# Converting weight blocks in pairs, and a new order of the opening, in a fused attention and two-layer kernel

## The chip, the cores and the metric
The kernel runs on one core of a Trainium2 chip. The metric is device microseconds (us) of one execution, as a median of runs; smaller is better. The engines are TensorE (PE in the profile; its weight loads are PEld), VectorE (DVE), ScalarE (ACT), GpSimd (POOL) and SyncE (SP), which here only issues transfers (DMA). Each engine works through its own list of instructions strictly in the order in which the program lays them down, and waits at an instruction whose inputs aren't there yet.

## The reference, cut to what matters
```python
# attention: 4 batches, 8 heads, 576 positions, 64 per head; position i sees i-63 .. i
scores = scale * q @ k.T ; scores[outside window] = -1e9 ; attn = softmax(scores) ; o = attn @ v
x = o as 2304 tokens x 512
# first layer: w_in 512 x 2048, w_out 2048 x 512
g = softplus(x @ w_in) ; x2 = g @ w_out
# second layer: w_gate, w_val 512 x 1536, w_out 1536 x 512
y = (sigmoid(x2 @ w_gate) * (x2 @ w_val)) @ w_out
```
The weights arrive in double precision.

## The kernel before, in words
Queries are taken in groups of 64 positions (36 groups, 9 per batch); a group needs 128 keys, two neighbouring blocks of 64. Tokens go through the first layer in five blocks of 512, 384, 384, 512 and 512. Block 0 consists of groups 0 to 7, called near; their whole attention has to be done before the first projection (`m1_proj`, tile `h<-xt,w`) can start. I call the time up to that first projection the opening. Later groups' attention is slipped in between the projections of the block before theirs.

Every fp32 matmul of the two layers is made of three passes over a high and a low part (`mm3`, lines 349 to 351 before). So each block of weights, 128 x 512 values, has to be turned from the raw double bits into such a pair: `w_load` (SP, 512 KB), `w_scale` (ACT, L115), `w_shift`, `w_sign`, `w_low` (DVE, L120, L124, L129), `w_hi` (ACT, L135, writes the high part) and `w_lo` (POOL, L140, the difference). The first layer has 32 such blocks (16 of `w1`, 16 of `w2`), which are converted during the opening and block 0 and then stay in 32 slots `w0` to `w31`. The blocks of `wg` and `wv` are converted next, summed and split (`c_sums`, `c_hi`, `c_lo`) and sent back to memory (`c_send`) for the second layer; I call one wg block with its wv block a combination. There are 12. The 12 blocks of `wo` come last.

The attention of a group: `att_scores` (PE, L250), `att_max` (DVE, L259, L262), `att_exp` (ACT, L274, four exponentials with their sums), `att_sum` (DVE, L279, L280), `att_norm` (POOL, L285), `att_transpose` (PE, L293), `att_copy` (ACT, L322), `att_values` (PE, L331), `att_hi` (ACT, L339) and `att_lo` (DVE, L344), which write the block's input `xt`. For the near groups before, queries and keys are loaded apart: each even group takes its keys from the tiles of its two neighbours, by two half-wide matmuls per pair of heads.

The order of everything up to the second layer comes from a planner, `lead_in`: each step has a rank (a slot of the matmul sequence with small offsets), an engine, a duration and the steps that it depends on (`traits`), and the planner goes through a list of engines' free times and lays down what can start first, by rank among those within `SLACK`. In it a load is taken to land 0.85 us after the bytes before it and its own have passed. After the projection of each chunk come softplus (`m1_act`, ACT, L368), `g_hi` (ACT, L375) and `g_lo` (DVE, L381), and then the output matmuls (`m1_out`, tile `acc<-g,w`). Softplus and the exponential need different tables on ACT; changing costs an `ACT_TABLE_LOAD`.

Of the kernel before, what the change touches and what calls it, by code (L numbers as in the profile page):

```python
# [28 lines left out]
FLYING, SWITCH = 10, 1.3  # L29
AHEAD = 160  # L30
STB, PB, VB, GB, RB, BB = 3, 2, 2, 3, 3, 3
# [3 lines left out]
def tile_kernel(ctx: ExitStack, tc: tile.TileContext, qk, vt, w1, w2, wg, wv, wo, out):  # L35
# [68 lines left out]
    raw_t, bits_t, w_t = {}, {}, {}  # L104

    def w_load(i):
        t = main.tile([P, 2 * DM], U32, tag="raw", name="raw", bufs=RB)
        nc.sync.dma_start(out=t, in_=allw[i][1])
        raw_t[i] = t.rearrange("p (n two) -> p n two", two=2)
# [3 lines left out]
    def w_scale(i):  # L113
        t = main.tile([P, DM], U32, tag="bits", name="bits", bufs=BB)
        nc.scalar.activation(out=t.bitcast(F32), in_=raw_t[i][:, :, 1].bitcast(F32), func=AF.Copy, scale=2.0 ** -112)  # L115
        bits_t[i] = t
# [5 lines left out]
    def w_sign(i):  # L122
        t, r = bits_t[i], raw_t[i]
        nc.vector.scalar_tensor_tensor(out=t, in0=r[:, :, 1], scalar=0x80000000, in1=t, op0=ALU.bitwise_and,  # L124
                                       op1=ALU.bitwise_or)

    def w_low(i):
        t, r = bits_t[i], raw_t.pop(i)
        nc.vector.scalar_tensor_tensor(out=t, in0=r[:, :, 0], scalar=29, in1=t, op0=ALU.logical_shift_right,  # L129
                                       op1=ALU.bitwise_or)  # L130

    def w_hi(i):
        t, slot = bits_t[i].bitcast(F32), place[i]
        w = wpool.tile([P, 2, DM], F32R, tag=f"w{slot}", name=f"w{slot}", bufs=1)
        nc.scalar.copy(out=w[:, 0, :], in_=t)  # L135
        w_t[allw[i][0]] = w

    def w_lo(i):
        t, w = bits_t.pop(i).bitcast(F32), w_t[allw[i][0]]
        nc.gpsimd.tensor_tensor(out=w[:, 1, :], in0=t, in1=w[:, 0, :].bitcast(F32), op=ALU.subtract)  # L140
# [5 lines left out]
    def c_load(i):  # L146
        w_load(i)
        send_t[i] = raw_t[i].rearrange("p n two -> p (n two)").bitcast(F32R).rearrange("p (e n) -> p e n", e=2)

    def c_sums(f):  # L150
        g, v = (bits_t[len(seq1) + 2 * f + k].bitcast(F32) for k in range(2))
        x = main.tile([P, DM], F32, tag="bits", name="sums", bufs=BB)
        a11, a12, a21, a22, s1, s2 = (t[:, k * HC:(k + 1) * HC] for t in (g, v, x) for k in range(2))
        nc.vector.tensor_tensor(out=s1, in0=a21, in1=a22, op=ALU.add)
        nc.vector.tensor_tensor(out=s2, in0=s1, in1=a11, op=ALU.subtract)
        nc.vector.tensor_tensor(out=a21, in0=a11, in1=a21, op=ALU.subtract)
        sum_t[f] = x

    def c_sum4(f):
        g = bits_t[len(seq1) + 2 * f].bitcast(F32)  # L160
        nc.vector.tensor_tensor(out=g[:, HC:], in0=g[:, HC:], in1=sum_t[f][:, HC:], op=ALU.subtract)

    def c_part(f, part):
        i = len(seq1) + 2 * f
        if part == "x":
            t = sum_t[f]
            if (f, part) not in send_t:
                r = main.tile([P, 2 * DM], U32, tag="raw", name="sumr", bufs=RB)
                send_t[f, part] = r.bitcast(F32R).rearrange("p (e n) -> p e n", e=2)
            return t, send_t[f, part], 4 * DM  # L170
        if part == "s4":
            t = bits_t[i]
            return t.bitcast(F32)[:, HC:], t.bitcast(F32R).rearrange("p (e n) -> p e n", e=2), 6 * DM
        k = "av".index(part)
        return bits_t[i + k].bitcast(F32), send_t[i + k], 2 * k * DM
# [5 lines left out]
    def c_lo(f, part):  # L181
        t, o, _ = c_part(f, part)
        nc.gpsimd.tensor_tensor(out=o[:, 1, :], in0=t, in1=o[:, 0, :].bitcast(F32), op=ALU.subtract)
# [25 lines left out]

    def v_load(g):  # L210
        b, i = divmod(g, NSEQ)
        c0, c1 = max(i - 1, 0) * Q, (i + 1) * Q
        if g < NG0:
            vp = wpool.tile([P, 2, DM], F32, tag=f"w{NSLOT - 1 - NG0 - g}", name="vp0", bufs=1)
            v, p_t[g] = vp[:, 0, :], vp[:, 1, :].rearrange("p (j k) -> p j k", j=NPAIR)
# [6 lines left out]
    def first_tile(g):  # L222
        if g not in qk_t:
            qk_t[g] = wpool.tile([P, 2, NPAIR, P], F32, tag=f"w{NSLOT - 1 - g}", name="qk0", bufs=1)
        return qk_t[g]

    def q_load(g):
        nc.sync.dma_start(out=first_tile(g)[:, 0], in_=qk[g, :, 0])

    def k_load(t):  # L230
        nc.sync.dma_start(out=first_tile(2 * t + 1)[:, 1], in_=qk[2 * t + 1, :, 1])

    def qk_load(g):
        t = late["apool"].tile([P, 2, NPAIR, P], F32, tag="qk", name="qk", bufs=2)
# [3 lines left out]
    def att_scores(g):  # L238
# [3 lines left out]
        if g >= NG0 or g % 2:  # L242
            parts = [(0, w, t[:, 1])]
        elif g:
            parts = [(0, Q, qk_t[g - 1][:, 1, :, Q:]), (Q, Q, qk_t[g + 1][:, 1])]
        else:
            parts = [(0, Q, qk_t[1][:, 1])]
        for j in range(NPAIR):
            for at0, n, keys in parts:
                nc.tensor.matmul(out=s[:, j, at0:at0 + n], lhsT=t[:, 0, j, :], rhs=keys[:, j, :n], start=True,  # L250
                                 stop=True)
        s_t[g] = s

    def att_max(g):
        w = width(g)
        s = s_t.pop(g)
        p = p_t[g] if g < NG0 else late["apool"].tile([P, NPAIR, P], F32, tag="p", name="p", bufs=PB)
# [169 lines left out]
    def x2_hi(s, k, kc):  # L427
        c = wpool.tile([P, 2, DM], F32R, tag=f"w{2 * k + kc}", name="xc", bufs=1)[:, :, :HALF]
# [9 lines left out]
    def tmp(s, f, k):  # L438
        if (s, f, k) not in tmp_t:
            i = (s * NF2 + f) % 2  # L440
            t = wpool.tile([P, 2, DM], F32, tag=f"w{NSLOT - NF2 - 6 + 3 * i + k}", name=f"t{k}", bufs=1)
# [151 lines left out]
    def weight(i, t):  # L593
        at(t - 2, 50, w_load, i)
# [5 lines left out]
        at(t + 2, -19, w_lo, i)  # L600

    for i in range(len(seq1)):
# [4 lines left out]
    def used_last(slot):  # L607
        (kind, f), _ = seq1[slot]
        return pos[m1_proj if kind == "w1" else m1_out, NB1 - 1, f]

    for f in range(NF2):
        t, i = COMBO0 + int(COMBO * f), len(seq1) + 2 * f
        for k in range(2):
            at(t - 2 + k, -60, c_load, i + k)
            at(t + k, -20, w_scale, i + k)
            at(t + k + 1, -20, w_shift, i + k)
            at(t + k + 1, -19, w_sign, i + k)
            at(t + k + 1, -18, w_low, i + k)
# [6 lines left out]
    for f in range(NF2):  # L625
# [3 lines left out]
        assert used_last(place[i]) < t + 4 < pos[m2_out, 0, f, 0]  # L629
# [43 lines left out]
    for g in range(NG0):  # L673
        t = int(first + RG * g)
        attention(g, t, False)
        if g % 2 == 0:
            at(t - 4, -63, k_load, g // 2)
        at(t - 4, -62, q_load, g)
# [12 lines left out]
    def traits(fn, a, *rest):  # L691
        early = fn.__name__.startswith(("att", "v_")) and a < NG0
        f = rest[-1] if rest else a
        wide = 1.0 if fn.__name__.startswith(("att", "v_")) and width(a) == P else 0.6
        if fn in (w_load, c_load):
            freed = (w_low, a) if fn is w_load else (c_send, (a - NSLOT) // 2, "av"[a % 2])
            f = (a - NSLOT) // 2 - 1
            deps = [(w_load, NSLOT - 1)] if f == -1 else [(c_hi, f, "x")] if f >= 0 else []
            return "sp", 512, deps * (fn is c_load or a == WO_AT), [("raw", RB, freed)]
        if fn is qk_load:  # L700
            return "sp", 512, [], [("qk", 2, (att_scores, a))]
# [208 lines left out]
```

## Time and profile before
| what | us |
|---|---|
| median of 3 runs (944.41 to 946.98) | 945.0 |
| profiled execution, whole | 943.91 |
| its span, first to last instruction | 942.1 |
| PE busy in the span | 898.3 (95%) |
| DVE, ACT, POOL busy | 512.0, 401.4, 251.1 |

The profiled execution's time is 1.81 us over its span. PE is the engine that sets the end: its busy time, with the weight loads beside it, is 95% of the span. The 43.8 us in which it is not busy, and the stretches in which its clock is granted at half, are what a better order can give back. The clock of the span's first 15 us is not in the record and is shown as full there; durations of single matmuls tell more in that stretch.

### The profile page before, as it was taken

How to read it: one execution, taken by the hardware profiler on the slowest of the kernel's cores; microseconds unless marked ns; L12 is line 12 of the kernel's file. 1: busy time of each engine (PE TensorE's matmuls, PEld its weight loads, DVE VectorE, ACT ScalarE, POOL GpSimd, SP SyncE). 2: the span in 40 equal slices, each digit the busy share in tenths (PEclk: the TensorE clock that was granted, in tenths of full speed). 3: DMA queues.
4: the chain of work that ended last, by engine and by line, in shares of the span. 5: the costliest groups of instructions: out<-in, count | busy, mean ns of one | idle time of the engine just before them, and what ended most of it. 6: DMA issues, size and time to landing. Idle time of an engine off the chain costs nothing.

```text
span 942.1 us, 13708 instructions
## 1 busy us (share of the span) xinstructions
PE 898.3 (95%) x5024; PEld 805.2 (85%) x5024; DVE 512.0 (54%) x922; ACT 401.4 (43%) x928; POOL 251.1 (27%) x232
## 2 busy tenths in 40 slices
PE   6589998899999998999999899999999999999998
PEld 6468877899889987888888799998999998999996
DVE  3787877465556565654211558666545446444443
ACT  4767666563766566543312332334222224222222
POOL 2443344232232222231100223334211114111111
PEclk9899999999999999999999999999999999999999
DMA  9445654866777576674002656554564444644441
GB/s 325 141 149 179 206 178 142 267 214 219 267 250 271 209 261 201 216 263 169 1 1 101 246 205 237 188 208 166 219 232 169 163 158 163 218 157 157 157 157 67
DMA packets 56643, 176.54 MB, mean 187 GB/s; under 512 B 6144, under 2 KB 21248, under 8 KB 51968
## 3 DMA queue, kind: packets, MB, share of 16 engines
q1 hardware_dynamic: 56576, 175.66, 53.2%
q8 instruction: 40, 0.66, 0.3%
q14 instruction: 27, 0.22, 0.1%
HBM read 138.67 MB, written 36.96 MB: 186 GB/s over the span
## 4 chain that ended last, share of the span: by engine, by line
PE 76%; DMA 7%; DVE 7%; ACT 4%; issue 3%; POOL 1%; SPq 1%; ACTq 0%; DVEq 0%; POOLq 0%
PE h L349 14%; PE h L350 14%; PE h L351 14%; PE acc L351 9%; PE acc L349 9%; PE acc L350 9%; DMA raw<-in_wv 2%; PE at L250 2%; DMA wcd<-raw 2%; PE at L351 1%; DVE t L457 1%; PE at L350 1%; PE at L349 1%; PE at L331 1%; DMA qk<-in_qk 1%
## 5 line engine op out<-in xcount | busy, mean ns | idle before, releaser
L457 DVE TENSOR_TENSOR t<-h,t 128x384 f32<-128x384 f32 x216 | 117.0, 556 | 169.1 <-PE h L351 160.9
L349 PE MATMUL h<-xc,wc 128*128 128x384 f32 x504 | 170.1, 337 | 1.3 <-DVE t L457 0.9
L350 PE MATMUL h<-xc,wc 128*128 128x384 f32 x504 | 170.4, 338 | 0.0
L351 PE MATMUL h<-xc,wc 128*128 128x384 f32 x504 | 169.8, 337 | 0.0
L463 POOL TENSOR_TENSOR g<-t,g 128x384 fp32r<-128x384 f32 x72 | 74.5, 1035 | 297.9 <-ACT g L462 297.9
L349 PE MATMUL h<-xt,w 128*128 128x512 f32 (+1 forms) x320 | 120.7, 377 | 11.6 <-DVE g L381 10.2
L349 PE MATMUL acc<-g,w 128*128 128x512 f32 (+1 forms) x320 | 120.6, 377 | 2.6 <-ACT w L135 2.6
L381 DVE TENSOR_TENSOR g<-h,g 128x512 fp32r<-128x512 f32 (+1 forms) x80 | 50.7, 635 | 132.1 <-ACT g L375 131.9
L351 PE MATMUL acc<-g,w 128*128 128x512 f32 (+1 forms) x320 | 119.1, 372 | 1.2 <-POOL w L140 1.2
L351 PE MATMUL h<-xt,w 128*128 128x512 f32 (+1 forms) x320 | 118.4, 370 | 0.8 <-POOL w L140 0.8
L350 PE MATMUL h<-xt,w 128*128 128x512 f32 (+1 forms) x320 | 118.4, 370 | 0.5 <-DVE xt L344 0.5
L350 PE MATMUL acc<-g,w 128*128 128x512 f32 (+1 forms) x320 | 118.6, 371 | 0.0
L349 PEld LDWEIGHTS h<-xc,wc 128*128 128x128 f32 x504 | 95.1, 189 | 10.7 <-DVE t L457 1.9
L462 ACT CAST g<-t 128x384 fp32r<-128x384 f32 x72 | 37.0, 514 | 156.6 <-DVE t L457 139.7
L350 PEld LDWEIGHTS h<-xc,wc 128*128 128x128 f32 x504 | 95.1, 189 | 6.5
L140 POOL TENSOR_TENSOR w<-bits,w 128x512 fp32r<-128x512 f32 x44 | 59.4, 1352 | 136.7 <-ACT w L135 84.2
L351 PEld LDWEIGHTS h<-xc,wc 128*128 128x128 f32 x504 | 95.2, 189 | 0.0
L368 ACT ACTIVATE h<-h 128x512 f32<-128x512 f32 (+1 forms) x80 | 43.2, 540 | 112.5 <-PE h L351 112.3
L349 PEld LDWEIGHTS h<-xt,w 128*128 128x128 f32 x320 | 60.5, 189 | 21.0 <-DVE g L381 11.6
L115 ACT ACTIVATE bits<-raw 128x512 f32<-128x512 f32 x68 | 45.4, 671 | 63.4 <-DMA raw<-in_wv 22.8
L349 PEld LDWEIGHTS acc<-g,w 128*128 128x128 f32 x320 | 60.9, 190 | 11.5 <-ACT w L135 3.5
L351 PEld LDWEIGHTS acc<-g,w 128*128 128x128 f32 x320 | 60.7, 190 | 9.9 <-POOL w L140 2.1
(93 smaller groups left out, 1520.3 us busy)
## 6 DMA issues: line engine op xcount, KB each, us to landing
wc<-wcd SPq DMA_DIRECT2D x36, 1792.0 KB, 7.3
raw<-in_w SPq DMA_DIRECT2D x32, 512.0 KB, 3.8
qk<-in_qk SPq DMA_DIRECT2D x28, 512.0 KB, 4.6
wcd<-raw SPq DMA_DIRECT2D x24, 512.0 KB, 3.8
v<-in_vt SPq DMA_DIRECT2D x25, 256.0 KB, 3.6
raw<-in_wg SPq DMA_DIRECT2D x12, 512.0 KB, 4.6
raw<-in_wv SPq DMA_DIRECT2D x12, 512.0 KB, 4.8
wcd<-sumr SPq DMA_DIRECT2D x12, 512.0 KB, 5.6
```

What stands on the lines that cost most here:

```text
L115: nc.scalar.activation(out=t.bitcast(F32), in_=raw_t[i][:, :, 1].bitcast(F32), func=AF.Copy, scale=2.0 ** -112)
L140: nc.gpsimd.tensor_tensor(out=w[:, 1, :], in0=t, in1=w[:, 0, :].bitcast(F32), op=ALU.subtract)
L250: nc.tensor.matmul(out=s[:, j, at0:at0 + n], lhsT=t[:, 0, j, :], rhs=keys[:, j, :n], start=True, stop=True)
L331: nc.tensor.matmul(out=o[h * Q:(h + 1) * Q, j, :], lhsT=v[:w, (2 * j + h) * Q:(2 * j + h + 1) * Q], rhs=pt[:w, h, j], start=True, stop=True)
L349: nc.tensor.matmul(out=o, lhsT=lh, rhs=rh, start=first, stop=False)
L350: nc.tensor.matmul(out=o, lhsT=lh, rhs=rl, start=False, stop=False)
L351: nc.tensor.matmul(out=o, lhsT=ll, rhs=rh, start=False, stop=last)
L368: nc.scalar.activation(out=t, in_=t, func=AF.Softplus)
L381: nc.vector.tensor_tensor(out=g[:, 1, :n], in0=t, in1=g[:, 0, :n].bitcast(F32), op=ALU.subtract)
L457: nc.vector.tensor_tensor(out=out, in0=a, in1=b, op=op)
L462: nc.scalar.copy(out=g[:, 0, :HALF], in_=t)
L463: nc.gpsimd.tensor_tensor(out=g[:, 1, :HALF], in0=t, in1=g[:, 0, :HALF].bitcast(F32), op=ALU.subtract)
```

## The change
It has four parts.

1. Two neighbouring blocks (2u, 2u+1) are converted by one instruction per step: `w_scale`, `w_shift`, `w_sign`, `w_low` and `w_hi` now work on 128 x 1024 values. Only `w_lo` stays per block, and it may go to POOL or to DVE, whichever the planner sees done first (`EITHER`); so may `c_lo`. The blocks of `wo` stay single.
2. Slots become pairs (`w0` to `w15`, each two of the old). Raw bits and the values in work of most pairs of the first layer lie in slots whose weights come later (`raw_slot`, `bits`), instead of in three small buffers each.
3. Near groups load queries and all 128 keys at once (`qk_load`, 512 KB per group, 4 MB in all instead of 3 MB), and each has four matmuls of full width (64 keys for group 0).
4. The planner: ranks are in microseconds; those of the near attention and of the first layer's weights are worked back from when the matmul that uses them is due; a load is taken to land 1.5 us later than before (`MARGIN`); a table change counts as work of ACT; loads keep their order.

```diff
+OPEN = 34.0
+FLYING, SWITCH, MARGIN = 10, 1.3, 1.5
+EITHER, HALVES = (("pool", 1.29), ("dve lock", 0.69)), (("pool", 0.75), ("dve lock", 0.42))
-STB, PB, VB, GB, RB, BB = 3, 2, 2, 3, 3, 3
+STB, PB, VB, GB, RB = 3, 2, 2, 3, 2
...
+    def raw_slot(u):
+        return u + 4 if u < 4 else u % 4 + 10 if u < 12 and u % 4 > 1 else None
...
+    def bits(i):
+        if i not in bits_t:
+            u, n = i // 2, size(i)
+            if u < 3:
+                t = main.tile([P, 2, DM], U32, tag="g", name="bits", bufs=GB)
+            elif 4 <= u < 14:
+                slot = 14 + u % 4 // 2 if u < 12 else 15
+                t = pair(2 * slot, -20 - u // 2, U32, 2 * DM)[:, u % 2].rearrange("p (c n) -> p c n", c=2)
+            else:
+                t = main.tile([P, 2, DM], U32, tag="bits", name="bits", bufs=1)
...
     def w_scale(i):
-        nc.scalar.activation(out=t.bitcast(F32), in_=raw_t[i][:, :, 1].bitcast(F32), func=AF.Copy, scale=2.0 ** -112)
+        nc.scalar.activation(out=bits(i).bitcast(F32), in_=raw(i, 1).bitcast(F32), func=AF.Copy, scale=2.0 ** -112)
...
-    def w_lo(i):
-        t, w = bits_t.pop(i).bitcast(F32), w_t[allw[i][0]]
-        nc.gpsimd.tensor_tensor(out=w[:, 1, :], in0=t, in1=w[:, 0, :].bitcast(F32), op=ALU.subtract)
+    def w_lo(i, engine):
+        w = w_t[allw[i][0]]
+        t = bits_t[i - i % size(i)][:, i % size(i)].bitcast(F32)
+        eng = nc.gpsimd if engine == "pool" else nc.vector
+        eng.tensor_tensor(out=w[:, 1], in0=t, in1=w[:, 0].bitcast(F32), op=ALU.subtract)
...
     def qk_load(g):
-        t = late["apool"].tile([P, 2, NPAIR, P], F32, tag="qk", name="qk", bufs=2)
+        if g < NG0:
+            t = pair(NSLOT - NG0 + g, -1, F32, 2, NPAIR, P)[:, g % 2]
+        else:
+            t = late["apool"].tile([P, 2, NPAIR, P], F32, tag="qk", name="qk", bufs=2)
...
         for j in range(NPAIR):
-            for at0, n, keys in parts:
-                nc.tensor.matmul(out=s[:, j, at0:at0 + n], lhsT=t[:, 0, j, :], rhs=keys[:, j, :n], start=True,
-                                 stop=True)
+            nc.tensor.matmul(out=s[:, j, :w], lhsT=t[:, 0, j, :], rhs=t[:, 1, j, :w], start=True, stop=True)
...
+            if near or fn.__name__.startswith("w_") and a < NSLOT:
+                if fn is att_lo:
+                    due[key] = min(due.get(key, OPEN), OPEN - 2.9 * (NG0 - 1 - a))
+                us = 2 + us / 400 if kind == "sp" else us + 0.1
+                nodes[key][0] = due[key] - us
...
-                done[key] = dma + 0.85
+                done[key] = dma + 0.85 + MARGIN
```

ACT, from its first exponentials on (`vp` and `w_114` to `w_126` hold near groups' probabilities, `bits<-raw` is `w_scale`, `pt` is `att_copy`, `xt` is `att_hi`). Before:

```order
L274 ACTIVATE vp_129,st<-vp_129,st 128x64 x4
L115 ACTIVATE bits<-raw 128x512
L274 ACTIVATE vp_136,st<-vp_136,st 128x128 x4
L274 ACTIVATE vp_140,st<-vp_140,st 128x128 x4
L322 COPY pt<-acc_211 64x512
L274 ACTIVATE vp_142,st<-vp_142,st 128x128 x4
L115 ACTIVATE bits<-raw 128x512 x2
```

and now:

```order
L297 ACTIVATE w_114,st<-w_114,st 128x64 x4
L297 ACTIVATE w_114,st<-w_114,st 128x128 x4
L297 ACTIVATE w_120,st<-w_120,st 128x128 x4
L345 COPY pt<-acc_176 64x512
L345 COPY pt<-acc_201 128x512
L297 ACTIVATE w_120,st<-w_120,st 128x128 x4
L362 CAST xt<-at 128x4x64 x2
```

No `w_scale` stands among the first groups' exponentials any more; the first one now follows the exponentials of group 6.

SP, the loads from the middle of the opening on (`vp`, `w_126` and `w_197` by L254 are values of near groups, `in_w` are weight blocks). Before:

```order
L218 DMA vp_129<-in_vt 64x512
L231 DMA qk_131<-in_qk 128x512
L228 DMA qk_133<-in_qk 128x512
L228 DMA qk_131<-in_qk 128x512
L218 DMA vp_136<-in_vt 128x512
L108 DMA raw<-in_w 128x1024
L218 DMA vp_140<-in_vt 128x512
```

and now:

```order
L127 DMA w_158<-in_w 128x1024 x2
L254 DMA w_126<-in_vt 128x512
L254 DMA w_197<-in_vt 128x512 x2
L127 DMA w_228<-in_w 128x1024 x2
L127 DMA w_255<-in_w 128x1024 x2
L127 DMA w_297<-in_w 128x1024 x2
L254 DMA v<-in_vt 128x512
```

The first weight block was load 15 and is now load 16, but all eight near groups' keys and queries and two later groups' stand ahead of it, and weight loads come two by two.

ACT at the first projections (`h_520`, `h_539` before and `h_465`, `h_487`, `h_518` now are the first chunks; `p` are probabilities of groups 8 and 9; `w_508`, `w_504` and the like are weights, written by `w_hi`). Before:

```order
L274 ACTIVATE p,st<-p,st 128x128 x4
L274 ACTIVATE p,st<-p,st 128x64 x4
L135 CAST w_552<-bits 128x512
L115 ACTIVATE bits<-raw 128x512
L368 ACT_TABLE_LOAD
L368 ACTIVATE h_520<-h_520 128x512
L375 CAST g<-h_520 128x512
L368 ACTIVATE h_539<-h_539 128x512
```

and now:

```order
L391 ACTIVATE h_465<-h_465 128x512
L398 CAST g<-h_465 128x512
L168 CAST w_504<-bits 128x2x512
L391 ACTIVATE h_487<-h_487 128x512
L297 ACT_TABLE_LOAD
L297 ACTIVATE p,st<-p,st 128x128 x4
L297 ACTIVATE p,st<-p,st 128x64 x4
L398 CAST g<-h_487 128x512
L391 ACT_TABLE_LOAD
L391 ACTIVATE h_518<-h_518 128x512
L168 CAST w_560<-bits 128x2x512
L168 CAST w_568<-bits 128x2x512
```

The exponentials of groups 8 and 9 moved from ahead of the first softplus to behind the second, at the price of two more table loads, and the third and fourth pair's `w_hi` stand behind them.

## Rows read from the trace of the kernel before

**Rows 1.** Windows: stretch, busy us by engine (instructions), mean granted clock, DMA share, GB/s.
```profile
0.00:46.28 46.28, 29.97 (x264) 27.07 (x265) 27.13 (x57) 26.73 (x93) 15.02 (x23) 0.89 0.68 231
46.28:60.00 13.72, 9.94 (x34) 7.53 (x35) 11.75 (x20) 9.87 (x27) 6.13 (x5) 0.88 0.58 197
110.00:160.00 50.00, 45.29 (x227) 35.71 (x227) 35.82 (x58) 35.04 (x79) 21.41 (x16) 0.97 0.49 162
160.00:300.00 140.00, 131.47 (x925) 127.21 (x924) 78.80 (x162) 81.99 (x212) 40.12 (x36) 1.00 0.72 244
300.00:500.00 200.00, 197.53 (x1059) 167.62 (x1058) 91.43 (x168) 92.22 (x206) 43.26 (x39) 0.99 0.48 162
```

**Rows 2.** Waits of PE over the span: total us, times, longest.
```profile
PE h L349 <- DVE g L381: 10.2, 4, 3.3
PE acc L349 <- ACT w L135: 3.6, 3, 1.7
```

**Rows 3.** Timeline of ACT in the opening: start, us, [idle before <-releaser].
```profile
15.66 0.67 ACT L115 ACTIVATE bits<-raw 128x512 f32<-128x512 f32 x1 [6.29 <-DMA raw<-in_w]
16.23 0.39 ACT L274 ACTIVATE vp<-vp,st 128x128 f32<-128x128 f32 x1
...
19.32 0.56 ACT L322 COPY pt<-acc 64x512 f32<-64x512 f32 x1
...
26.90 0.36 ACT L339 CAST xt<-at 128x256 fp32r<-128x256 f32 x1
```

**Rows 4.** Timeline of PE, opening to the end of the weights' stage.
```profile
4.96 1.94 PE L250 MATMUL acc<-qk,qk 128*128 128x64 f32 x8 [4.96 <-DMA qk<-in_qk]
6.70 2.02 PE L250 MATMUL acc<-qk 128*128 128x128 f32 x8
...
24.83 1.06 PE L250 MATMUL acc<-qk 128*128 128x128 f32 x8
...
46.28 0.49 PE L349 MATMUL h<-xt,w 128*128 128x512 f32 x1 [1.35 <-ACT xt L339]
...
56.10 0.76 PE L349 MATMUL h<-xt,w 128*128 128x512 f32 x1 [3.28 <-DVE g L381]
...
112.63 0.39 PE L349 MATMUL acc<-g,w 128*128 128x512 f32 x1
...
115.35 0.39 PE L349 MATMUL h<-xt,w 128*128 128x512 f32 x1
```

**Rows 5.** Windows of the opening, columns as in rows 1.
```profile
10.00:15.00 5.00, 5.00 (x25) 4.86 (x25) 1.80 (x5) 0.00 (x0) 0.61 (x1) 1.00 1.05 360
19.00:22.00 3.00, 3.00 (x16) 2.67 (x18) 2.90 (x8) 3.00 (x14) 1.54 (x2) 0.50 1.04 405
```

**Rows 6.** DVE, groups by form, 0 to 160 us: count, busy us, mean ns.
```profile
L124 DVE SCALAR_TENSOR_TENSOR bits<-raw,bits 128x512 uint32<-128x512 uint32 x32 | 27.1, 847 | 0.8
L120 DVE TENSOR_SCALAR bits<-bits 128x512 uint32<-128x512 uint32 x33 | 20.7, 626 | 2.1 <-ACT bits L115 2.0
L381 DVE TENSOR_TENSOR g<-h,g 128x512 fp32r<-128x512 f32 x16 | 10.9, 688 | 15.7 <-ACT g L375 15.6
...
L381 DVE TENSOR_TENSOR g<-h,g 128x384 fp32r<-128x384 f32 x1 | 0.6, 551 | 0.0
```

**Rows 7.** ACT and POOL, groups by form, 0 to 160 us.
```profile
L115 ACT ACTIVATE bits<-raw 128x512 f32<-128x512 f32 x34 | 22.8, 675 | 27.7 <-DMA raw<-in_w 22.6 <-POOL w L140 4.7 <-DMA raw<-in_wg 0.4
...
L375 ACT CAST g<-h 128x512 fp32r<-128x512 f32 x16 | 9.4, 588 | 0.4
...
L140 POOL TENSOR_TENSOR w<-bits,w 128x512 fp32r<-128x512 f32 x32 | 43.5, 1363 | 74.6 <-ACT w L135 74.6
```

**Rows 8.** Timelines of POOL and DVE around 20 us.
```profile
20.02 1.07 POOL L285 TENSOR_TENSOR vp<-vp,st 128x512 f32<-128x512 f32 x1 [0.55 <-ACT pt L322]
...
20.22 1.41 DVE L124 SCALAR_TENSOR_TENSOR bits<-raw,bits 128x512 uint32<-128x512 uint32 x1
...
35.29 0.88 DVE L120 TENSOR_SCALAR bits<-bits 128x512 uint32<-128x512 uint32 x1
...
38.27 0.42 DVE L120 TENSOR_SCALAR bits<-bits 128x512 uint32<-128x512 uint32 x1
```

**Rows 9.** Timeline of ACT around 184 us, at a combination's `w_scale`.
```profile
183.97 0.67 ACT L115 ACTIVATE bits<-raw 128x512 f32<-128x512 f32 x1 [4.08 <-DMA raw<-in_wv]
184.65 1.28 ACT L368 ACT_TABLE_LOAD   x1
...
186.46 0.48 ACT L375 CAST g<-h 128x384 fp32r<-128x384 f32 x1
```

## What I predicted
> **What bounds the kernel now.** I read the stretches first, then what PE waited for, then the timelines around those waits. The windows show PE at work nearly throughout from 160 us on, and the losses gathered early [rows 1]: it is busy for 29.97 of the first 46.28 us, and that work is attention alone, which the later stretches hide between projections. After it 3.78 us are idle up to 60 us, 4.71 between 110 and 160, 8.53 between 160 and 300, 2.47 between 300 and 500. [...]
>
> The first projection starts at 46.28 us [rows 4]. Why so late is on ACT [rows 3]: it stood still for 6.29 us, from 9.37 to 15.66, at a `w_scale` whose raw block hadn't landed, while the second group's exponentials, queued behind it, could have run. From there the opening goes at ACT's pace: two groups' exponentials take from 16.23 to 19.32, so 1.55 us each. In the later stretches the longest sum of PE's waits is for `g_lo` [rows 2]: 10.2 us in four waits, one of them 3.28 at 56.10 [rows 4], behind the exponentials of groups 8 and 9. The timeline of ACT shows how the other three (6.9 together) come about [rows 9]: a combination's `w_scale` waits 4.08 us for its load, and a softplus that PE needs stands behind it, with a table load of 1.28.
>
> **The opening.** Removed: ACT's wait of 6.29, eight half-wide matmuls of each even group but the first (halved in number), and conversions between the first groups. Moved: weights' loads behind the groups' loads.
>
> ACT's own work is the lower bound. Up to the last `att_hi` its list holds eight groups of exponentials (8 x 1.55 = 12.4), eight copies (0.56 each, 4.5), eight casts (0.36 each, 2.9) [rows 3], three wide `w_scale` and one wide `w_hi`. A `w_scale` of 128 x 512 takes 675 ns; a cast costs 108 ns more at 512 than at 384 columns [rows 7, 9], 0.84 ns per column, so 1024 columns make 1.11 us. With four of these (4.4) the sum is 24.2. The first group's exponentials end at 9.37 as before, so the rest ends at 9.37 + 24.2 - 1.55 = 32.0 if ACT never waits.
>
> It will wait. Four groups' scores now stand ahead of the first transpose on PE, and at the low level a group takes 1.8 us (eight matmuls start at 6.70 and run 2.02, against 1.06 at 24.83 [rows 4]). So the fourth ends at about 12.1; group 4's scores and the second transpose follow at 15.6, while ACT is through with group 2 at 13.4: 2.2 us. Groups 5 to 7 pass exponentials, 1.07 of normalising on POOL [rows 8], transpose, copy and values one after another with less beside them, for which I set 2.3. That gives 36.5. If PE stays low through all eight groups, five of them cost 0.9 more each: 41.
>
> Loads can hide. Ahead of the first pair's landing lie 4.2 MB of near queries and keys, 1.05 of two later groups, 1.2 of values, 1.05 of weights: 7.5 MB, which at 360 to 405 GB/s [rows 5] take 19 to 21 us, landing at 22 to 24; its `w_scale` comes up on ACT at about 25. At 300 GB/s it would be 28, and the start 3 us later, within the upper bound. So the first projection starts at 36.5 (32 to 41), which is -9.8 us (-14.3 to -5.3).
>
> **Block 0's weights.** An uncontended two-operand DVE step takes 688 ns at 512 columns and 551 at 384 [rows 6], 1.07 ns per column, so 1.24 at 1024; the wide `w_sign` and `w_low` aren't in the trace. Bounds: 0.69, as if width were free, and 2 x 0.847 = 1.69, twice the narrow mean with its waits [rows 6]; I take 1.24, the nearest row's slope. A wide `w_shift` lies between 0.42 [rows 8] and 2 x 0.626; I take 0.69. A `w_lo` on DVE is 0.69 like `g_lo`. [...]
>
> Per pair that is 0.69 + 2 x 1.24 + about 1.7 of its two `w_lo` on DVE (27 of 32 blocks are there now) x 0.69 = 4.3 us of DVE; with `g_lo` (0.69) and a share of attention (0.85) 5.9. Before, a pair cost DVE 2 x (0.626 + 2 x 0.847) = 4.6 and POOL 2 x 1.36. PE's pace is two stages of 2.72 (112.63 to 115.35 [rows 4]) and 0.8 of attention, 6.2 per pair. So DVE keeps up, closely, and the two waits on weights between 110 and 160 should go.
>
> What is late next is at the start, where no lead has built up. The second pair's `w_lo` stands on DVE behind the third pair's two wide steps and a `g_lo`: third chunk 1.5 us late. Then ACT does exponential table, exponentials of groups 8 and 9, softplus table (1.28, 2.9, 1.28 [rows 9, 3]) before the third pair's `w_hi`: fourth chunk 1.9 us late. Each may drop the clock; I put 2.5 us for that. New losses 5.9, old ones 3.78 + 4.71 + 1.6 + 1.5 = 11.6, so -5.7 (-11.6 to +4, the latter if DVE runs 0.3 us per pair behind PE).
>
> Here rows speak of a limit: a DVE step that starts 0.20 us into a normalising on POOL lasts 1.41 instead of about 0.69 [rows 8]. [...]
>
> **Combinations.** The wide `w_scale` waits for both loads, where before half of the work could start after one. But the planner now takes a load to land 1.5 us later, and in the order four stages of matmuls stand between the second load and its `w_scale`. Against 4.08, 1.5 is not all. I take half of the 8.53 idle us as gone: -4 (-8.5 to +28, see the rival). **Second layer:** its matmuls, single `wo` blocks and POOL's splits stay; pair slots free a few steps later, which the lead of the planner covers: 0 (+-2).
>
> **Sum.** 943.9 of the profiled execution - 9.8 - 5.7 - 4 = 924.4; the median of the runs shown is 1.1 above that execution, so 925.5.
>
> **Rivals.**
> *The two-load wait on ACT, slower.* At each of twelve combinations `w_scale` waits for the second load, which SP issues only after the previous combination's sends have freed the buffer, since the ring now has two buffers of a pair. Each wait costs PE what it cost at 56.10's kin, about 2.9, in all 35, where before 6.9 were lost so: +28. With the opening's and block 0's -15.5 that is 957. For it: three such waits in the trace already. Against: 1.5 us of margin, and some 25 us between combinations for a round of about 18. From eight such waits on the gain is gone. 6%.
> *The opening hardly gains.* PE low for long, or ACT waiting at transposes where it waited at a load: start at 41, block 0 gives 0, combinations -2: 945 - 5.3 - 2 = 938. For it: ACT's lists are strict, and copies of later groups stand ahead of exponentials. 22%.
> *DVE becomes the bound in block 0.* [...] For it: DVE 85% busy from 46 to 60 us [rows 1]. [...] 12%.
> *Everything fits.* ACT never waits, no early weight is late: -14.3 - 9 - 8: 914. 8%.
>
> **How the numbers follow.** My forecast has 52%, with 919 to 932 as its own range. About 0.3% (942.2 to 947.8) is what can't be told from no change. From 914 to 941 the first, the second and third rival and part of the last are held, about 85%. Faster takes all but the slower rival and the worst of the second: 0.90, same 0.04, slower 0.06.
>
> **What would show it.** Right: no load among the releasers of ACT before 20 us; first `h` matmul between 34 and 39; a wide `w_low` at 1.2 us; no wait of PE on `w` between 90 and 150; PE waits at the third and fourth chunk. Wrong: an ACT wait on `raw<-in_wv` over 2 us in most combinations, a first projection after 41, or DVE without a gap and PE waiting on it through block 0.

## The result and the profile after

The changed kernel takes 915.18 us (median of 4 runs, 914.86 to 917.56), the one before 944.70 beside it (941.24 to 946.98, 4 runs). The ratio is 0.9696, with a 95% interval from 0.9662 to 0.9730. The forecast was 925.5, in a range from 914 to 941: the direction was right, and the gain is 29.5 us where I had 19.5. The result lies near the fast end of that range and outside the 919 to 932 that I had given as the forecast's own.

I divide the span at the starts of the first projection of each token block. Each figure is the length of that part, in us; the last two rows are experiments told below.

| kernel | opening | block 0 | 1 | 2 | 3 | 4 | second layer |
|---|---|---|---|---|---|---|---|
| before | 46.3 | 108.2 | 83.0 | 84.1 | 100.8 | 87.0 | 428.5 |
| after | 34.0 | 99.7 | 83.6 | 80.3 | 97.2 | 87.0 | 427.0 |
| difference | -12.3 | -8.6 | +0.6 | -3.8 | -3.6 | 0.0 | -1.5 |
| margin alone, on before | 45.8 | 110.4 | 77.5 | 81.3 | 97.6 | 87.0 | 427.0 |
| last pair earlier, on after | 33.7 | 99.4 | 77.4 | 80.0 | 97.2 | 87.0 | 428.6 |

The second layer's part ends with the last matmul; what comes after it grew from 4.2 to 4.8 us. So the parts add to -28.6, which is what the span lost (942.1 to 913.5). Each row is one profiled execution, and parts move with small changes of order: block 1 takes 83.0 us in the kernel before and 79.7 in the first experiment, whose edit concerns the opening alone. Differences of one or two us in one part say little.

The windows of the changed kernel answer to [rows 1] (same columns); its first two end at the first projections of blocks 0 and 1:

```profile
0.00:34.00 34.00, 22.85 (x241) 20.29 (x241) 21.40 (x46) 24.45 (x85) 9.90 (x19) 1.00 0.98 356
34.00:133.60 99.60, 96.67 (x530) 79.16 (x530) 86.82 (x119) 70.39 (x127) 12.65 (x10) 0.98 0.54 193
...
110.00:160.00 50.00, 47.41 (x256) 41.07 (x255) 35.21 (x52) 27.21 (x53) 6.34 (x5) 0.93 0.48 161
160.00:300.00 140.00, 140.00 (x1001) 135.78 (x1000) 79.32 (x160) 83.51 (x219) 17.17 (x17) 1.00 0.70 232
```

The same stretch of block 0 in the kernel before:

```profile
46.28:154.50 108.22, 99.73 (x528) 80.01 (x529) 83.73 (x133) 73.90 (x166) 44.45 (x34) 0.97 0.54 181
```

PE's idle time in block 0 fell from 8.49 to 2.93 us, and between 160 and 300 us from 8.53 to nothing. One stretch got worse: 110 to 160 us shows a mean clock of 0.93, where it was 0.97. The waits of PE say why (total us, times, longest), against [rows 2]:

```profile
PE acc L316 <- POOL w L308: 3.4, 3, 1.5
PE acc L372 <- ACT w L168: 2.9, 2, 1.9
...
PE h L372 <- ACT w L168: 0.8, 1, 0.8
PE acc L374 <- DVE w L176: 0.7, 1, 0.7
```

No wait of a first-layer projection for `g_lo` is left. Waits of output matmuls for a weight's high part (`acc<-g,w` at L372) were there before too, 3.6 us in three; now they are 2.9 in two. PE's timeline, against [rows 4]:

```profile
8.48 3.66 PE L271 MATMUL acc<-w 128*128 128x128 f32 x16 [0.21 <-DMA w<-in_qk]
...
12.42 1.06 PE L271 MATMUL acc<-w 128*128 128x128 f32 x8
...
33.97 0.48 PE L372 MATMUL h<-xt,w 128*128 128x512 f32 x1
...
43.02 0.50 PE L372 MATMUL h<-xt,w 128*128 128x512 f32 x1 [0.81 <-ACT w L168]
...
50.47 1.20 PE L316 MATMUL at<-ident,p 128*128 128x128 f32 x8 [1.45 <-POOL p L308]
...
137.79 0.50 PE L372 MATMUL acc<-g,w 128*128 128x512 f32 x1 [1.90 <-ACT w L168]
...
139.39 0.79 PE L374 MATMUL acc<-g,w 128*128 128x512 f32 x1 [0.69 <-DVE w L176]
...
141.26 0.63 PE L372 MATMUL acc<-g,w 128*128 128x512 f32 x1
```

The reader is to see three things. A group's eight score matmuls take 1.06 us from 12.42 on, so PE is at its high level there (3.66 for the two groups before is the low one). The third chunk's projection waits 0.81 us at 43.02, and two transposes wait 1.45 at 50.47. At 137.79 and 139.39 PE waits 2.59 in all, and then matmuls that take 0.39 elsewhere take 0.63: the granted clock is 0.51 as a mean from 138.1 to 145.0, the low level. ACT, before that wait:

```profile
132.32 1.28 ACT L297 ACT_TABLE_LOAD   x1
133.62 0.40 ACT L297 ACTIVATE p<-p,st 128x128 f32<-128x128 f32 x1
...
136.71 1.03 ACT L168 CAST w<-bits 128x1024 fp32r<-128x1024 f32 x1
137.76 1.28 ACT L391 ACT_TABLE_LOAD   x1
```

The `w_hi` of the last pair of blocks (30 and 31) stands on ACT behind a table load and eight exponentials of two later groups.

### The profile page after: what moved, and what is told of

Same layout as the page of the kernel before. It is cut to its first block, busy times and chain, and to the rows that moved or that the text cites. A ratio compares the mean times of both kernels' runs of the same rounds, so it can differ in the third digit from the quotient of the medians.

```text
span 913.5 us, 13423 instructions
## 1 busy us (share of the span) xinstructions
PE 888.2 (97%) x5000; PEld 796.9 (87%) x5000; DVE 521.5 (57%) x903; ACT 398.5 (44%) x886; POOL 170.3 (19%) x167
## 5 line engine op out<-in xcount | busy, mean ns | idle before, releaser
L480 DVE TENSOR_TENSOR w<-h,w 128x384 f32<-128x384 f32 x216 | 116.9, 555 | 168.3 <-PE h L374 160.5
L372 PE MATMUL h<-w,wc 128*128 128x384 f32 x504 | 169.3, 336 | 1.3 <-DVE w L480 0.9
L373 PE MATMUL h<-w,wc 128*128 128x384 f32 x504 | 169.8, 337 | 0.0
L374 PE MATMUL h<-w,wc 128*128 128x384 f32 x504 | 169.3, 336 | 0.0
L486 POOL TENSOR_TENSOR g<-w,g 128x384 fp32r<-128x384 f32 x72 | 74.5, 1034 | 296.7 <-ACT g L485 261.6
L372 PE MATMUL acc<-g,w 128*128 128x512 f32 (+1 forms) x320 | 120.0, 375 | 1.9 <-ACT w L168 1.9
L372 PE MATMUL h<-xt,w 128*128 128x512 f32 (+1 forms) x320 | 120.9, 378 | 0.8 <-ACT w L168 0.8
L485 ACT CAST g<-w 128x384 fp32r<-128x384 f32 x72 | 37.0, 513 | 156.4 <-DVE w L480 139.6
L372 PEld LDWEIGHTS h<-w,wc 128*128 128x128 f32 x504 | 94.6, 188 | 10.7 <-DVE w L480 1.9
L373 PEld LDWEIGHTS h<-w,wc 128*128 128x128 f32 x504 | 94.5, 188 | 6.5
L374 PEld LDWEIGHTS h<-w,wc 128*128 128x128 f32 x504 | 94.7, 188 | 0.0
L372 PEld LDWEIGHTS acc<-g,w 128*128 128x128 f32 x320 | 60.5, 189 | 10.4 <-ACT w L168 2.2
L372 PEld LDWEIGHTS h<-xt,w 128*128 128x128 f32 x320 | 60.8, 190 | 9.2 <-ACT w L168 1.2
L373 PEld LDWEIGHTS h<-xt,w 128*128 128x128 f32 x320 | 60.7, 190 | 8.2 <-DVE xt L367 1.0
L374 PEld LDWEIGHTS h<-xt,w 128*128 128x128 f32 x320 | 60.6, 189 | 8.2 <-DVE w L176 0.4
```

What stands on the lines that cost most here:

```text
L372: nc.tensor.matmul(out=o, lhsT=lh, rhs=rh, start=first, stop=False)
L373: nc.tensor.matmul(out=o, lhsT=lh, rhs=rl, start=False, stop=False)
L374: nc.tensor.matmul(out=o, lhsT=ll, rhs=rh, start=False, stop=last)
L480: nc.vector.tensor_tensor(out=out, in0=a, in1=b, op=op)
L485: nc.scalar.copy(out=g[:, 0, :HALF], in_=t)
L486: nc.gpsimd.tensor_tensor(out=g[:, 1, :HALF], in0=t, in1=g[:, 0, :HALF].bitcast(F32), op=ALU.subtract)
```

## The experiments

Each was timed against the kernel before on the same chip; ratios are to that kernel, with 95% intervals.

### What made the opening late

*ACT's wait alone.* To before I added one dependency: the first `w_scale` comes behind the third group's exponentials. If the wait of [rows 3] made the opening late, that should bring most of its gain.

```diff
+            order += [(att_exp, 2)] * (a == 0)
```

> The kernel before with one dependency more: the first w_scale stands behind the exponentials of group 2, so ACT no longer waits for its raw block with groups 1 and 2 queued behind. Theory A (the opening was late because of that wait on ACT): the first projection comes 4 to 6 us earlier, at 40 to 42 us, and the time falls by about 5, to 940. Rival B (PE's half-wide score matmuls at the low clock level set the opening): the first projection stays within 1.5 us of 46.3 and the time at 944 to 945.

943.42 us, ratio 0.9986 (0.9957 to 1.0015); first projection at 45.2, so 1.1 earlier. The projection is where the rival has it; the rival's reason is not tested by this. The first exponentials do run on, but later weight steps wait in the same way, and PE waits behind them. ACT, then PE, in this kernel:

```profile
16.89 0.67 ACT L115 ACTIVATE bits<-raw 128x512 f32<-128x512 f32 x1
19.23 0.68 ACT L115 ACTIVATE bits<-raw 128x512 f32<-128x512 f32 x1 [1.67 <-DMA raw<-in_w]
21.89 0.66 ACT L115 ACTIVATE bits<-raw 128x512 f32<-128x512 f32 x1 [1.98 <-DMA raw<-in_w]
...
29.13 0.68 ACT L115 ACTIVATE bits<-raw 128x512 f32<-128x512 f32 x1 [2.25 <-DMA raw<-in_w]
```

```profile
24.70 0.83 PE L293 MATMUL acc<-ident,vp 128*128 128x128 f32 x4 [3.03 <-ACT pt L322]
...
30.42 1.08 PE L293 MATMUL acc<-ident,vp 128*128 128x128 f32 x4 [3.84 <-ACT pt L322]
```

So the one long wait that I had named is not by itself the cause: taken away, it comes back in pieces at the next three blocks. Up to 46 us ACT waits 7.9 us for raw blocks here, where it was 8.3 before. The experiment moved ACT's waits for loads and did not remove them, so it does not show what they cost together.

*Own keys alone* (on before, full-width scores):

```diff
-        nc.sync.dma_start(out=first_tile(g)[:, 0], in_=qk[g, :, 0])
+        nc.sync.dma_start(out=first_tile(g), in_=qk[g])
```

> The kernel before with near groups that load all their own keys and do full-width score matmuls; conversions, buffers and planner as before. Theory A (ACT's wait is what counts): first projection within 2 us of 46.3, since a w_scale still stands ahead of group 1's exponentials; time 943 to 946. Rival B (the score matmuls and PE's clock): PE reaches its high level some 4 us earlier and the first projection comes at 40 or before; time about 938.

941.30, ratio 0.9957 (0.9919 to 0.9995); first projection at 45.5, as theory A has it, though the time is below its range. PE is through with five groups' scores at 13 us and then waits 7.15 us for a normalising, up to 20.14, since ACT still stands at a `w_scale` for 7.35, up to 16.29.

*Ranks worked back alone* (on before; the loop over `due` of the changed kernel, with the old steps):

```diff
+                nodes[key][0] = due[key] - us
```

> The kernel before with ranks in microseconds, those of the near attention and of the first-layer weights worked back from the using matmul, and nothing else of the change. In the changed kernel these ranks made the first projection 7.8 us earlier (34.0 against 41.8). If they do so by themselves: first projection at 37 to 40, but weights are late behind it, as three raw buffers and POOL's w_lo stay; time 936 to 942. Rival (the ranks need pairs and wide matmuls to gain): first projection after 43, time within 3 us of before or slower.

938.92, ratio 0.9932 (0.9895 to 0.9970); first projection at 44.0, 2.3 earlier, between the two expectations. ACT still waits 3.88 us for a load, up to 22.07, and PE 5.52 behind it, up to 24.55.

*The changed kernel without its ranks* (the line above left out):

> The changed kernel without the ranks worked back from the using matmul: near attention and first-layer weights are ranked by their slot only. Theory A (what stands ahead of the exponentials on ACT decides): as the list of ACT has no w_scale before the exponentials of group 4 here either, the first projection comes at 34 to 37; time 915 to 919. Rival C (the ranks make the gain): first projection at 40 or later, or waits on weights of over 5 us in block 0; time 922 or more.

915.26, ratio 0.9677 (0.9650 to 0.9703). The first projection is at 41.8, 7.8 later than in the changed kernel, as rival C has it; the time is not, as block 0 is 3.2 shorter, and block 1 is 77.4, without the stall at 137.79. Block 1 starts at 138.3 here and at 133.6 in the changed kernel, so 4.7 of the 7.8 are left by then. DVE and PE in this opening:

```profile
21.01 1.15 DVE L153 TENSOR_SCALAR bits<-bits 128x1024 uint32<-128x1024 uint32 x1 [0.59 <-ACT bits L149]
22.19 1.23 DVE L157 SCALAR_TENSOR_TENSOR bits<-w,bits 128x1024 uint32<-128x1024 uint32 x1
23.45 1.22 DVE L162 SCALAR_TENSOR_TENSOR bits<-w,bits 128x1024 uint32<-128x1024 uint32 x1
24.59 0.41 DVE L367 TENSOR_TENSOR xt<-at,xt 128x256 fp32r<-128x256 f32 x1
```

```profile
18.98 0.69 PE L354 MATMUL at<-pt,w 128*64 128x64 f32 x16
...
25.06 1.12 PE L354 MATMUL at<-pt,w 128*64 128x64 f32 x16 [2.74 <-DVE xt L367]
```

```profile
23.00:41.83 18.83, 11.61 (x104) 9.67 (x104) 16.17 (x27) 14.04 (x28) 2.73 (x3) 0.50 1.03 389
```

A group's `att_lo` stands behind a pair's three wide steps on DVE; PE waits 2.74 us for it, and its matmuls then take 1.12 instead of 0.69. The granted clock stays at 0.50 up to the first projection (the third figure from the end), where it is 1.00 throughout the changed kernel's opening from 15 us on. So the 7.8 us hold both the order and the lower clock that came with it, and I can't part them. The ranks keep most weight steps out of the near attention's way on every strict list, not on ACT alone: with them DVE's first wide step starts at 25.18.

*The changed kernel with shared keys* (even near groups take their keys from both neighbours again, 3 MB instead of 4):

```diff
+        if g < NG0 and g % 2 == 0:
+            nc.sync.dma_start(out=t[:, 0], in_=qk[g, :, 0])
...
+                parts = [(0, Q, qk_t[g - 1][:, 1, :, Q:]), (Q, Q, qk_t[g + 1][:, 1])]
```

> The changed kernel with keys of even near groups taken from their neighbours again, by two half-wide matmuls (3 MB loaded instead of 4). Theory A: loses only what PE's extra matmuls cost, first projection at 34 to 37 against 34.0, time 915 to 918. Rival B: the low clock level lasts to 15 us as in the kernel before, first projection at 38 to 41, time 919 to 922. Group 1 now stands ahead of group 0 in the lists, which both would let pass.

911.18, ratio 0.9630 (0.9604 to 0.9657). First projection at 36.6, as theory A has it: own keys are worth 2.6 us of opening. But block 0 is 2.2 shorter here (97.5), so block 1 starts at 134.1 against 133.6, and little of the 2.6 is left by then. The whole is 4.0 faster than the changed kernel, since in this order the stall at 137.79 does not occur (block 1 is 77.4).

### What made block 0 shorter

*Width.* The changed kernel, each wide step given as two of 512:

```diff
+        for c in range(size(i)):
+            nc.vector.tensor_scalar(out=t[:, c], in0=t[:, c], scalar1=3, scalar2=None, op0=ALU.logical_shift_left)
```

> The changed kernel with the same order, slots and loads, but every wide step (w_scale, w_shift, w_sign, w_low, w_hi) given out as two of 512 columns one behind the other. Theory A (the order is what gains): a step of 1024 columns costs two of 512 less about 0.15 us, five steps a pair, of which three on DVE and two on ACT, so 0.3 to 0.5 us per pair and engine; block 0 loses 1 to 3 us, the time is 916 to 918. Rival D (fewer instructions are what lets DVE keep up): DVE falls behind PE in block 0, waits on weights of 5 us and more, time 921 or more.

913.62, ratio 0.9665 (0.9626 to 0.9705); block 0 is 101.8, so width is worth 2.1 us there, as theory A has it. That the whole comes out 1.6 lower than the changed kernel is again block 1 (79.7), where part of the stall is gone.

*DVE's share of `w_lo`.* The changed kernel with all of it on POOL:

```diff
+EITHER, HALVES = (("pool", 1.29),), (("pool", 0.75),)
```

> The changed kernel with every w_lo and c_lo on POOL, as before the change, and the planner told so. [...] Rival E (DVE's share of w_lo does nothing): within 2 us of 915.

918.65, ratio 0.9722 (0.9682 to 0.9762), 3.5 above the changed kernel, where rival E has up to 2. Block 0 is 109.1 (+9.4), the first projection is not later (33.8), and block 1 is free of the stall (76.8). *The same share on before* (five blocks of six on DVE):

```diff
+        eng = nc.vector if i < NSLOT and i % 6 != 5 else nc.gpsimd
```

> The kernel before with w_lo of five in six first-layer blocks on DVE instead of POOL, planner told so. In the changed kernel DVE's share of w_lo made block 0 9.7 us shorter. If it does so by itself: block 0 at 99 to 103 instead of 108.2, time 937 to 941. Rival (here three raw buffers set the pace of the weights): block 0 within 3 us of 108, time 942 to 947.

939.19, ratio 0.9936 (0.9907 to 0.9965): block 0 is 97.6 (-10.6), but the opening is 4.4 longer (I did not follow why), so block 1 starts 6.3 earlier than before. The windows of block 0 in these two, all on POOL first, then DVE's share on before:

```profile
33.80:142.90 109.10, 102.45 (x539) 81.42 (x539) 78.30 (x100) 72.84 (x142) 52.74 (x38) 0.95 0.53 185
```

```profile
50.60:148.20 97.60, 97.10 (x529) 80.27 (x529) 81.93 (x147) 66.57 (x134) 13.87 (x11) 0.97 0.56 189
```

PE is idle for 6.65 us in the one and 0.50 in the other, while POOL's busy time is 52.74 against 13.87. So it matters which engine does `w_lo`, in either kernel. Through which waits is shown only in part: in the first, 2.3 us of PE's waits end on a `w_lo` on POOL, 1.4 on a `w_hi`, and 2.7 on normalisings before which POOL itself had been idle; its clock is also lower (0.95 against 0.98 over block 0). In the second, the later start gives the conversions 4.4 us more of a lead, so not all of the -10.6 need be due to the share.

*Room in empty slots.* The changed kernel with raw bits in a ring of two pairs and, after the first three pairs, one buffer for values in work:

```diff
     def raw_slot(u):
-        return u + 4 if u < 4 else u % 4 + 10 if u < 12 and u % 4 > 1 else None
+        return None
```

> The changed kernel without tiles in empty slots: raw pairs go through the ring of two alone, values in work of the fourth pair and later through one buffer. Theory I (room for loads ahead is a large part of the gain): a pair must be wholly converted before the next one's w_scale, a round of some 8 to 10 us against PE's 6.2 per pair; block 0 takes 20 us or more above 99.7, time 930 or more. Rival (conversions' engines, not room, set the pace): block 0 within 6 us, time up to 920.

932.85, ratio 0.9864 (0.9815 to 0.9914). The opening is 32.9, block 0 is 125.5 (+25.8). Its windows and its longest wait of PE from 30 to 160 us:

```profile
33.00:158.40 125.40, 110.10 (x569) 87.03 (x570) 94.69 (x138) 82.74 (x165) 14.34 (x13) 0.93 0.57 194
```

```profile
PE h L372 <- ACT w L168: 9.3, 4, 2.8
```

Without room for pairs on the way, PE waits for weights through block 0, in four waits that end at 50.1, 96.3, 127.2 and 144.6. This is the largest loss of all the parts taken out, as theory I has it, and the prediction gave it no term. It is the price of two pairs of raw bits and one pair of values in work; which of the two runs short was not tried. The kernel before made do with 108.2 on three single buffers of each kind, so I take it that it is the pairs that need the room; that is not shown, as single blocks with slots as room were not run.

### The stall at 137.79

*The last pair earlier.* The changed kernel, the ranks of blocks 30 and 31 set 6 us ahead:

```diff
-                nodes[key][0] = due[key] - us
+                nodes[key][0] = due[key] - us - 6.0 * (not near and a >= NSLOT - 2)
```

> The changed kernel with the ranks of the last pair of first-layer blocks (30 and 31) 6 us earlier, so that its w_hi stands ahead of the exponentials of groups 14 and 15 on ACT instead of behind them. Theory A (PE's 2.6 us of waits at 137 to 139.4 and the 6.8 us at the low clock level behind them come from that order): both go, 5 to 6 us less, time 909.5 to 910.5. Rival: the exponentials, now later, delay a softplus or attention by as much, time 913 or more.

909.39 (908.12 to 912.10, 6 runs), ratio 0.9626 (0.9593 to 0.9659): the fastest of all, as theory A has it; its slowest run, 912.10, is below the changed kernel's fastest, 914.86. ACT in it, with the last pair's `w_hi` now ahead of the table load and the exponentials, then block 1:

```profile
128.96 1.05 ACT L168 CAST w<-bits 128x1024 fp32r<-128x1024 f32 x1 [3.33 <-DVE bits L162]
...
131.84 1.28 ACT L297 ACT_TABLE_LOAD   x1
```

```profile
133.10:210.50 77.40, 77.40 (x529) 75.32 (x529) 44.24 (x83) 44.20 (x110) 10.07 (x10) 1.00 0.63 209
```

PE has no gap there any more. The stall cost 6.2 us (83.6 against 77.4): 2.59 of waiting, about 3.3 by the clock (0.96 as a mean over the 83.6 us in the changed kernel), and 0.3 within the rounding of that mean.

### The combinations

*Margin alone*, on before:

```diff
-                done[key] = dma + 0.85
+                done[key] = dma + 0.85 + 1.5
```

> The kernel before with nothing changed but the 1.5 us by which the planner takes a load to land later. If the margin takes ACT's waits at the combinations away, the idle time of PE between 160 and 300 us falls from 8.5 to under 3 and the time by 5 or more, to 940 or less. If pairs and their own buffers took them away (the changed kernel without the margin kept none), blocks 1 to 3 stay within 3 us of what they took and the time within 4 us of the kernel before.

931.92, ratio 0.9861 (0.9811 to 0.9910), by this one number. Blocks 1 to 3 are 11.5 us shorter, the opening only 0.5, and block 0 is 2.2 longer. Between 160 and 300 us PE is idle for 1.39 us instead of 8.53. ACT's wait for the second load of a combination, from 150 to 520 us, in the kernel before and then with the margin:

```profile
ACT bits L115 <- DMA raw<-in_wv: 22.8, 7, 4.5
```

```profile
ACT bits L115 <- DMA raw<-in_wv: 5.9, 4, 2.5
```

*The changed kernel without it:*

```diff
-FLYING, SWITCH, MARGIN = 10, 1.3, 1.5
+FLYING, SWITCH, MARGIN = 10, 1.3, 0.0
```

> The changed kernel with loads taken to land 1.5 us earlier in the planner (MARGIN 0). Theory F (the margin is what took away the waits of ACT at the combinations, 8.5 idle us of PE between 160 and 300 before): some of them come back, 4 to 8 us in all, time 919 to 923. Rival G (pairs and the loads' order took them away): no PE wait over 1 us in blocks 1 to 4, time 914 to 917.

912.41, ratio 0.9658 (0.9611 to 0.9704): not slower. It is faster than the changed kernel only because the stall does not occur (block 1 is 77.9); block 1 starts 1.7 us later, and blocks 2 and 3 are the same within 0.5. ACT's same wait, in the changed kernel with and then without the margin:

```profile
ACT bits L149 <- DMA raw<-in_wv: 13.4, 6, 3.2
```

```profile
ACT bits L149 <- DMA raw<-in_wv: 23.0, 9, 4.5
```

and PE's windows without it:

```profile
160.00:300.00 140.00, 139.80 (x999) 135.75 (x998) 82.73 (x162) 82.99 (x208) 17.19 (x17) 1.00 0.69 231
```

ACT waits 9.6 us more without the margin, but PE is idle for 0.20 us in this stretch, and in blocks 1 to 4 no wait of PE over 1 us is left, as rival G has it. So the margin is enough in the old structure and not needed in the new one: two causes, each of which suffices. Which part of the new structure does it (buffers per pair, loads in order, table changes counted as work) was not tried.

## Why the prediction was right, and where it was wrong

**The opening: size off, and the wait that it starts from not the cause by itself.** I had -9.8, measured are -12.3. That ACT would be free of loads before 20 us held: its first wait for one ends at 24.01.

```profile
9.76 0.40 ACT L297 ACTIVATE w<-w,st 128x128 f32<-128x128 f32 x1 [0.83 <-DVE st L285]
...
12.01 0.40 ACT L297 ACTIVATE w<-w,st 128x128 f32<-128x128 f32 x1 [0.60 <-DVE st L285]
...
13.57 1.22 ACT L345 COPY pt<-acc 64x512 f32<-64x512 f32 x2
...
24.01 1.14 ACT L149 ACTIVATE bits<-w 128x1024 f32<-128x1024 f32 x1 [0.41 <-DMA w<-in_w]
...
33.39 0.38 ACT L362 CAST xt<-at 128x256 fp32r<-128x256 f32 x1
```

The step that failed is "Why so late is on ACT", as far as it names one wait: with that wait removed the start moved by 1.1 us, and as much waiting came back behind it. What the runs show to matter is that few weight steps stand in the near attention's way on any engine's list (7.8 us when taken out of the changed kernel) and that each group has its own keys (2.6). Put into the kernel before one at a time, these gave 2.3 and 0.8: in both, ACT still stood at a `w_scale` (3.88 and 7.35 us) with attention behind it. Both together in the kernel before were not run, and as they depend on each other, 7.8 and 2.6 need not add up to a share of the 12.3.

The term that was too large is the 4.5 us of waiting (2.2 and 2.3) that I added to the bound of 32.0: ACT's list ended at 33.77, so 1.8 of them came. At the copies of the first transposes, for which I had the 2.2, ACT does not wait at all, as PE was at its high level from about 12 us on.

**Block 0: the ledger right, the credit in the wrong place.** The old losses are 8.49 idle and 3.2 by the clock (0.97 over 108.22), together 11.7 against my 11.6 (the 1.6 and 1.5 for the clock in it are estimates from [rows 1]: 0.12 of 13.72 us and 0.03 of 50). The new ones are 2.93 and 2.0 (0.98 over 99.6), so 4.9 against my 5.9. The difference of these is -6.8 of the -8.6; the rounding of the clock column can hide about 1.0 of the rest, and 0.8 stays open. The chunks that I named were late, by less: 0.81 for the third instead of 1.5; at the fourth, two transposes by 1.45 instead of the projection by 1.9. Durations, by form, 0 to 160 us (count, busy us, mean ns), of DVE:

```profile
L176 DVE TENSOR_TENSOR w<-w,w 128x512 fp32r<-128x512 f32 x17 | 14.5, 884 | 1.2 <-ACT w L168 1.2
...
L157 DVE SCALAR_TENSOR_TENSOR w<-raw,w 128x1024 uint32<-128x1024 uint32 x6 | 7.3, 1220 | 0.1
...
L153 DVE TENSOR_SCALAR w<-w 128x1024 uint32<-128x1024 uint32 x10 | 6.8, 684 | 1.2 <-ACT w L149 1.2
```

and of ACT:

```profile
L168 ACT CAST w<-w 128x1024 fp32r<-128x1024 f32 x10 | 10.4, 1056 | 1.6 <-DVE w L162 1.6
...
L149 ACT ACTIVATE w<-raw 128x1024 f32<-128x1024 f32 x6 | 6.9, 1153 | 5.3 <-DMA raw<-in_w 2.5 <-POOL w L176 1.9 <-ACT pt L345 0.9
```

I had 1.24, 0.69 and 1.11 for the wide steps: measured are 1.22, 0.68 and 1.06 to 1.15. A `w_lo` on DVE was under-priced: 0.88 instead of 0.69. A pair then costs DVE 0.68 + 2 x 1.22 + 1.7 x 0.88 = 4.6 instead of 4.3, and still DVE did not become the bound that the third rival makes of it: PE waited once for a `w_lo` on DVE, 0.69 at 139.39. The limit that I read from [rows 8] shows in the kernel before (0 to 160 us) in 13 of its 64 `w_sign` and `w_low`: these started while POOL was at work and took 1.17 to 1.79, the others at most 0.69. In the changed kernel none of the 32 wide ones started so, and each took 1.21 to 1.23; what POOL's work would add to a wide step is not shown. The upper bound of +4 does not follow from my figures: 0.3 us for each of 16 pairs is 4.8, which makes -0.9 of the -5.7. What I priced at nothing, slots as room, is worth 25.8 us to this way of converting pairs.

**"No wait on `w` between 90 and 150": failed.** I had looked for what is late at the start, where no lead has built up, and not at the last pair, which the ranks, worked back to the moment of use, leave until then. It cost 6.2 us, and hid that the rest of the gain was larger still. That the time lies within my range is partly luck for this reason: without the stall, for which the prediction has no term, it is 909.39, below the range's fast end of 914.

**Combinations: half, in truth all.** Of the 8.53 idle us I took 4 as gone. That the two-load wait would reach PE, the rival on the slower side, did not happen: ACT waited 13.4 us in six, and PE was not idle between 160 and 300 us. (The 2.9 that I set for each such wait was above the 2.3 that 6.9 in three gives.) The margin, by which I argued, is one of two sufficient causes.

**Second layer.** 0 forecast, -1.5 in the traces (427.0 and 428.6 both occur among the variants of either kernel, so I make nothing of it).

The sum was 10.3 us short: 2.5 in the opening, 2.9 in block 0, 2.8 in blocks 1 to 3; the rest is the second layer and the step from a profiled execution to the median. The rival "everything fits" came closest (914), for other reasons than those it gives: ACT does wait, and early weights are late.

**Open.** What else shortened the opening and how much of it was the clock, whether raw bits or values in work need the slots, and which part makes late loads harmless to PE.

## What to carry to other kernels

A long wait in front of one instruction is not yet a cause: ask what stands behind it on the same strict list and on the next engine's, and whether the wait reappears there. A rank worked back from the use should leave some lead for steps that may fall behind a table change and a batch of exponentials; one such constant, 6 us for the last pair, gave 6.2 us here, more than own keys (2.6) and wide steps (2.1) gave in their parts. What a change gains in one part can be lost in the next, so compare the start of a later part too: without the ranks the opening is 7.8 us longer, and block 1 starts 4.7 later. An added margin on load landings in a planner is worth trying by itself first: alone it gave 13.8 us as a median, where the whole change gave 29.5.

## What the runs showed of the hardware that I had not expected

At the low level a score matmul of half the width took as long as one of the full width: eight with 64 columns 1.94 us, eight with 128 columns 2.02 [rows 4]. With each group's own keys PE reached its high level at about 12 us (a group's eight matmuls in 1.06 at 12.42). In the same kernel with shared keys it did so at about 18 us (two matmuls take 0.63 up to 17.45 and 0.39 from 18.18 on). The kernel before reached it at about 15, as 16 half-wide matmuls in 2.24 show, where 16 had taken 3.51 from 8.51 on; it was at the low one again after a wait of 2.19 (0.50 from 19 to 22 [rows 5]):

```profile
14.48 2.24 PE L250 MATMUL acc<-qk,qk 128*128 128x64 f32 x16
18.92 2.08 PE L250 MATMUL acc<-qk 128*128 128x128 f32 x8 [2.19 <-DVE vp L259]
```

A wait of 2.74 us in the opening without ranks and one of 1.90 with 0.69 later in the changed kernel came with a fall to the low level too (granted clock 0.50 and 0.51 behind them).

A `w_lo` of 128 x 512 took 0.88 us on DVE on average, and 1.41 to 1.64 on POOL in the kernel that leaves all of them there:

```profile
L176 POOL TENSOR_TENSOR w<-w,w 128x512 fp32r<-128x512 f32 x20 | 27.8, 1413 | 26.4 <-ACT w L168 26.4
L176 POOL TENSOR_TENSOR w<-bits,w 128x512 fp32r<-128x512 f32 x12 | 19.4, 1636 | 18.6 <-ACT w L168 18.6
```
